# DeltaNet and SiLU feed-forward: chunk 0's keys read in runs of 16 tokens, their lengths computed by GpSimd, the diagonal blocks taken from PSUM

## The chip, the core and the metric

The kernel runs on one core of one Trainium2 chip. The metric is device time in microseconds (us) of one execution, from repeated runs. The core's engines have their own instruction queues, run in order: TensorE (PE, its weight loads PEld), VectorE (DVE), ScalarE (ACT), GpSimd (POOL) and SyncE (SP), which here issues most of the DMA transfers.

## The reference

A DeltaNet recurrence over 768 tokens for 4 x 8 heads of dimension 48, then a feed-forward block with SiLU. All data are float32.

```python
batch, n_heads, seq, head_dim = (4, 8, 768, 48)
n_tokens, d_model, d_ff = (3072, 384, 2048)

k_n = k / (np.linalg.norm(k, axis=-1, keepdims=True) + 1e-06)
for t in range(S):
    kt, vt, bt = (k_n[:, :, t], v[:, :, t], beta[:, :, t, None])
    y[:, :, t] = np.einsum('bhd,bhde->bhe', q[:, :, t], state)
    v_old = np.einsum('bhde,bhd->bhe', state, kt)
    state = state + bt[:, :, :, None] * np.einsum('bhd,bhe->bhde', kt, vt - v_old)

x = y.transpose(0, 2, 1, 3).reshape(B * S, H * D)
h = x @ w_in
out = (h * (1.0 / (1.0 + np.exp(-h)))) @ w_out
```

## The kernel before

The sequence is cut into `NCH` = 6 chunks of `C` = 128 tokens. In a chunk the recurrence is turned into matrix products: the keys' scores (k times k transposed) of each head form a strictly triangular matrix of 128 x 128, of which each half of 64 tokens is solved by itself; in a half the two diagonal blocks of `T` = 32 tokens are inverted on VectorE, 128 blocks at once (32 heads x 4 blocks, one to a partition), and the corners between the blocks are joined on TensorE. Chunk 0 inverts in two steps: `invert_first` inverts blocks of 16 (`Q`), and the first joins (`corner`, `turned`, `straight`) make blocks of 32 of them; `merge_half` makes 64. The feed-forward of one chunk fills TensorE while the next chunk's recurrence is worked on. Its weights come by SP in pieces (`fetch_w_in`, `fetch_w_out`) and are rearranged on ScalarE, VectorE and GpSimd (`narrow`). The order of the instructions on each engine is that of the program text: `pin` ties each instruction behind the one before on its engine, `in_line` does it for SP's DMAs. The interleaving after the start is written by hand as strings of letters (`script`, `chunks`); later loads start at counts of TensorE's work (`loads`).

What the change touches is the start, where no feed-forward work exists yet:

- Keys. `load_k(0)` reads chunk 0's keys into `kbufs[0]` by `load_pair`: one token to a partition, all heads of a batch along the free axis, each head in a slot of `W` = 64 of which `D` = 48 are filled; the rest is set to zero on VectorE (L207). There are six transfers (L144), in pieces of 48 floats.
- Lengths. GpSimd squares the keys (`square`, L385), VectorE adds them (`add_squares`, L389) and runs `norm_steps`: an integer seed for the reciprocal root, three Newton steps, then length `n`, its reciprocal and -beta/length^2 (`step`), transposed so that it stands by block (L403 to L426). GpSimd then writes the lengths in the order of the values (`n_slot`, L440 and L443) and `step` on the diagonal of x (L1493).
- Scores. `turn` transposes the keys of one batch on TensorE (L510) and copies them from PSUM to `turned_kq` by VectorE or ScalarE (L522, L524); `first_score` makes the scores of that batch (L539) and copies them to `ap` (L554 by ScalarE, L557 by VectorE).
- Diagonal blocks. `diagonal_blocks` copies the 32 x 32 blocks out of `ap` into `stage`, 32 partitions a copy (six by ScalarE, L554, two by GpSimd, L560); `turn_diagonal` transposes them on VectorE so that each block lies on one partition (L578). Then `invert_first` begins (L697), with pairs of instructions L705 and L709, and ends with the transpositions L716 and L720. The joins begin with `corner` (L743, emptied by L750).
- Fillers. `busy(n)` issues n matmuls whose results nothing reads (L347). In the inversion's loop they stand behind steps 9, 11, 13 and 14:

```python
    for n in range(Q):
        done = next(inv)
        if n in (9, 11, 13):
            busy(2 if n < 13 else 1, done, Sync)
        if n in (6, 8, 10, 12):
            turn(1, n // 2 - 3, 0, M)
        if n == 14:
            busy(1, done, Sync)
```

Other names: `z` (`zbuf`) first holds chunk 0's queries; `sums_of_w`, `sums_of_g` and `stage` are large tiles whose room several things use in turn; `vf` holds a chunk's values; L467 multiplies them by the lengths; `state` is the recurrence's state, still zero in chunk 0. Lines L832 are `merge_half`, L866 and L910 the first products behind the joins, L1088 the feed-forward's first matmul.

## Time and profile before

| | |
|---|---|
| median of 3 runs | 634.13 us (633.98 to 637.14) |
| the profiled execution's own time | 633.96 us |
| its span, from the first to the last instruction | 631.8 us |
| mean granted TensorE clock | 0.989 |

All positions are in us from the span's start; 2.2 us of the profiled execution lie outside the span. A row of a timeline gives start, duration, engine, line, operation, output and inputs, shape and count; in square brackets stands how long the engine had been idle and what released it. A row of a group gives busy time and the mean of one in ns, then the idle time ahead of it. DMA rows give the KB of one issue and the median us from issue to landing. The granted clock is the share of TensorE's full speed that the chip allowed.

### The profile page before, as it was taken

What the parts mean: (1) busy time and instruction counts of PE and PEld (TensorE: products, weight loads), DVE (VectorE), ACT (ScalarE), POOL (GpSimd) and SP (SyncE); (2) the same over time, 40 slices, a digit from 0 to 9 for tenths busy, and PEclk for the clock granted to TensorE, in tenths of its full rate; (3) what the DMA queues carried; (4) which work ended last, traced back from release to release, by engine and by line L of the source; (5) the groups of instructions that cost most, each with busy time, mean ns of one, the idle gap of its engine ahead of it and who ended that gap; (6) DMA issues with size and microseconds to landing.
All of it is one profiled execution on the core that took longest, in us unless ns stands there. A gap on an engine that the chain in (4) does not pass through costs nothing.

```text
span 631.8 us, 21374 instructions
## 1 busy us (share of the span) xinstructions
PE 617.7 (98%) x9390; PEld 543.3 (86%) x9390; DVE 415.5 (66%) x927; ACT 226.7 (36%) x516; POOL 94.0 (15%) x101
## 2 busy tenths in 40 slices
PE   8889989999999999999999999999999999999997
PEld 5578778666799989989989989989989989988997
DVE  6886779999667974546975554976444983345432
ACT  4657873332441122451122451122452122454210
POOL 5234631335020020020020010020002000000000
PEclk9869999999999999999999999999999999999999
DMA  9656506350459360459141359433254024010011
GB/s 175 134 141 199 170 16 149 116 86 4 101 100 186 62 108 4 95 107 188 34 92 20 72 125 156 65 75 44 52 113 95 2 75 62 17 38 1 0 26 26
DMA packets 136941, 52.61 MB, mean 83 GB/s; under 512 B 108672, under 2 KB 130432, under 8 KB 136848
## 3 DMA queue, kind: packets, MB, share of 16 engines
q1 hardware_dynamic: 136512, 51.09, 39.6%
q8 instruction: 74, 1.21, 0.9%
q10 hardware_dynamic: 336, 0.15, 0.1%
q14 instruction: 19, 0.16, 0.1%
HBM read 39.09 MB, written 9.96 MB: 78 GB/s over the span
## 4 chain that ended last, share of the span: by engine, by line
PE 93%; SPq 2%; DMA 1%; issue 1%; ACT 1%; DVE 0%
PE phid L1088 34%; PE px L1200 17%; PE py L1200 13%; PE po L1132 5%; PE pb_c L866 3%; PE pa L539 2%; SPq L144 2%; PE pb_c L1303 2%; PE pb_c L854 2%; PE pyc L945 2%; PE pc L1303 2%; PE pb_c L1132 2%; PE pb_c L886 2%; PE pa L1303 1%; PE pyc L932 1%; PE px L808 1%
## 5 line engine op out<-in xcount | busy, mean ns | idle before, releaser
L1088 PE MATMUL phid<-xT,w_in 128*128 128x256 f32 x960 | 214.9, 382 | 1.9 <-issue 1.7
L1088 PEld LDWEIGHTS phid<-xT,w_in 128*128 128x128 f32 x960 | 180.2, 190 | 26.9 <-issue 2.8
L1098 ACT ACTIVATE gT<-phid 128x512 f32<-128x512 f32 x72 | 42.9, 597 | 115.2 <-PE phid L1088 106.2
L656 DVE SCALAR_TENSOR_TENSOR rank<-g,step,x 128x31 f32<-128x31 f32 (+15 forms) x124 | 49.8, 402 | 23.3 <-DMA g<-blocks 19.8
L1200 PE MATMUL px<-sums_of_w,sums_of_g 128*128 128x192 f32 x320 | 56.6, 329 | 0.0
L1200 PE MATMUL py<-w_out,sums_of_g 128*128 128x192 f32 x320 | 56.2, 328 | 0.0
L1200 PEld LDWEIGHTS px<-sums_of_w,sums_of_g 128*128 128x128 f32 x320 | 52.2, 190 | 0.4
L1200 PEld LDWEIGHTS py<-w_out,sums_of_g 128*128 128x128 f32 x320 | 52.3, 190 | 0.3
L661 DVE TENSOR_TENSOR x<-x,rank 128x31 f32<-128x31 f32 (+15 forms) x124 | 42.5, 342 | 4.3
L477 POOL TENSOR_TENSOR vf<-vf,n_slot 128x768 f32<-128x768 f32 x10 | 14.8, 1492 | 175.4 <-DMA vf<-in_v_dram 129.9
L1183 DVE TENSOR_TENSOR sums_of_g<-gT 128x384 f32<-128x384 f32 (+1 forms) x48 | 24.6, 540 | 14.6 <-ACT gT L1098 14.5
L498 DVE STREAM_TRANSPOSE kq<-stage 128x512 f32<-128x512 f32 x28 | 28.4, 1121 | 6.8 <-DMA stage<-in_q_dram 3.5
L554 ACT COPY xT<-pyc 48x128 f32<-48x128 f32 (+2 forms) x120 | 31.1, 259 | 1.6
L1211 DVE TENSOR_TENSOR o<-o,kept 128x192 f32<-128x192 f32 (+1 forms) x29 | 11.5, 425 | 26.7 <-ACT kept L1208 26.7
L560 POOL COPY g<-x 64x256 f32<-64x256 f32 x4 | 5.0, 1244 | 150.8 <-DVE x L664 150.8
L891 DVE TENSOR_TENSOR state<-state,pb_c 128x384 f32<-128x384 f32 x22 | 11.2, 550 | 24.6 <-PE pb_c L886 24.6
L866 PEld LDWEIGHTS pb_c<-vf,xi 64*64 64x64 f32 x736 | 23.3, 138 | 3.2 <-issue 2.3
L866 PE MATMUL pb_c<-vf,xi 64*64 64x48 f32 x736 | 24.9, 223 | 0.1
L1132 PE MATMUL po<-w_out,gT 128*128 128x384 f32 x64 | 23.7, 491 | 0.0
L1200 PE MATMUL py<-w_out,gT 128*128 128x192 f32 x128 | 23.4, 331 | 0.0
L859 DVE TENSOR_TENSOR vf<-vf,pb_c 128x384 f32<-128x384 f32 x22 | 11.2, 550 | 18.3 <-PE pb_c L854 15.5
L1200 PE MATMUL px<-w_out,gT 128*128 128x192 f32 x128 | 22.4, 327 | 0.0
(293 smaller groups left out, 1094.5 us busy)
## 6 DMA issues: line engine op xcount, KB each, us to landing
vf<-in_v_dram SPq DMA_DIRECT2D x48, 96.0 KB, 2.8
out_dram<-o SPq DMA_DIRECT2D x42, 96.0 KB, 2.2
w_out<-in_moe_w_in_dram SPq DMA_DIRECT2D x4, 768.0 KB, 5.0
sums_of_w<-in_moe_w_out_dram SPq DMA_DIRECT2D x4, 768.0 KB, 4.6
kb<-in_k_dram SPq DMA_DIRECT2D x12, 192.0 KB, 4.5
kb<-in_k_dram SPq DMA_DIRECT2D x24, 96.0 KB, 4.0
raw<-in_moe_w_in_dram SPq DMA_DIRECT2D x3, 768.0 KB, 6.8
blocks<-ap SPq DMA_DIRECT2D x32, 64.0 KB, 1.9
```

Of the source, the lines that this page charges most:

```text
L477: pin(nc.gpsimd.tensor_tensor(out=vf, in0=vf, in1=of, op=ALU.mult))
L498: pin(nc.vector.transpose(out=kqs[c, b][:, :, j, :].rearrange("p a (i m) -> p a m i", i=T), in_=src.rearrange("p a (m d) -> p a m d", d=D) ...
L554: return pin(nc.scalar.copy(to, of))
L656: pin(nc.vector.scalar_tensor_tensor(out=tv, in0=g[:, 0:m, m : m + 1].to_broadcast([P, m, n]), scalar=step[:, m : m + 1], in1=x[:, m : m + ...
L661: yield pin(nc.vector.tensor_tensor(out=x[:, 0:m, m:T], in0=x[:, 0:m, m:T], in1=tv, op=ALU.add))
L866: yield pin(nc.tensor.matmul(pz[rows, n * D : (n + 1) * D], lhsT=xis[g][rows, u * H + 2 * p + e, :], rhs=vfs[c][rows, hf, g * HB + u, p, : ...
L1088: pin(nc.tensor.matmul(ph[:, j * GT : (j + 1) * GT], lhsT=w_in[:, a, (2 * f + j) * P : (2 * f + j + 1) * P], rhs=xTs[c, hf][:, a, :], star ...
L1098: pin(nc.scalar.activation(out=hidden_of(c, hf, f), in_=ph[:], func=ACTF.Silu, scale=-0.5 if in_blocks(c) else 0.5))
L1132: pin(nc.tensor.matmul(pos[i][:, 0:DM], lhsT=hidden_of(0, hf, f // 2)[:, at : at + C], rhs=w_outs[f // HFF][:, f % HFF, :], start=(f == 0) ...
L1183: pin(nc.vector.tensor_tensor(out=sums_of_g[:, k, fs], in0=of[0], in1=of[1], op=op))
L1200: pin(nc.tensor.matmul(to, lhsT=at, rhs=quarter(f, *b) if isinstance(b, tuple) else sums_of_w[b][:, f], start=start and f == 0, stop=f == ...
L1303: pin(nc.tensor.matmul(to[:, i * GT : (i + 1) * GT], lhsT=left(a, slice(f, f + 1))[:, 0], rhs=right(b), start=start and i == 0 and n == 0, ...
```

## The change

1. Chunk 0's keys are first read by two transfers into `stage`, with 16 consecutive tokens of a head to a partition, so that one piece is 16 x 48 floats. Transfer e brings the heads of parity e (16 pairs of batch and head pair, 8 blocks of tokens each). `pad` copies them on chip into `kbufs[0]` in slots of 64, the even heads by ScalarE and the odd ones by VectorE, in two halves.
2. Four `first_turn` transpose them and write them by VectorE (the first) or ScalarE (the others) to `turned_kq`, where a token's place is reached with a stride of 16 floats. `turned_kq` now has keys and queries apart. The scores of two batches share a pair of banks, and which half of a bank holds which tokens is exchanged for some heads, so that the scores come out in the places that they had.
3. The diagonal blocks are made straight from PSUM: ScalarE multiplies one half by a 0/1 column (`halves`), VectorE adds the other half times the other column. The copies to `ap` come behind them.
4. The squares are made by ScalarE (first half) and GpSimd (second half). The sums are brought to one block a partition by four matmuls with a selecting matrix (`sel`, built from `ident` on VectorE). The root and the square of the length are computed by GpSimd in 14 instructions, with two refinements in place of three; VectorE takes the reciprocal and multiplies by beta, which it has transposed. ScalarE writes `step` on the diagonal. The lengths in the order of the values are written after the inversion.
5. `load_k(0)` comes again, behind `load_v(0)`, and brings the keys by token, as the state update needs them. Half of beta's issues move from ScalarE's queue to SP's, and ScalarE's table load (Silu) ahead of its own. Some memsets move between engines. Three fillers at the start read zeros only and don't wait for `ident`; of the six in the inversion's loop two are left.

```diff
-    for t in (kbufs[0], zbuf, kbufs[1]):
+    keys_0 = stage[:, 2 * BH * T + 4 * P :].rearrange("p (e x) -> p e x", e=2)
+    padded_0 = kbufs[0][:].rearrange("p b a e w -> p (b a e w)").rearrange("p (s e w) -> p s e w", e=2, w=W)
+    halves = const.tile([P, 2], FP32, name="halves")
+    for t in (kbufs[0], zbuf):
...
-    for g in range(2):
-        load_k(0, slice(HB * g, HB * (g + 1)))
+    for e in range(2):
+        issue(
+            keys_0[:, e],
+            k.rearrange("b (a e) (c i s) d -> e c (b a) i (s d)", e=2, c=NCH, i=2 * NB)[e, 0],
+        )
+    pin(nc.scalar.activation(out=seen[:], in_=seen[:], func=ACTF.Silu))
...
+    def pad(h):
+        for e, by in enumerate((by_act, by_dve)):
+            done = by(padded_0[:, h * STEPS // 2 : (h + 1) * STEPS // 2, e, 0:D], half_of(h)[:, e])
+        return done
...
+    def first_turn(h, by):
+        pt = bank(M, "pt")
+        for i in range(4):
+            pin(nc.tensor.transpose(
+                pt[:, C * i : C * (i + 1)], padded_0[:, 4 * h + i].rearrange("p e w -> p (e w)"), ident[:]
+            ))
+        to = turned_kq[:, 0].rearrange("p b a (i s) -> p s (b a i)", s=STEPS)[:, 4 * h : 4 * h + 4]
...
+    def first_step():
+        po = bank(M, "po")
+        for i in range(2):
+            for e in range(2):
+                pin(nc.tensor.matmul(
+                    po[:, STEPS * i : STEPS * (i + 1)], lhsT=sel[:, e, i].rearrange("p j g n f -> p (j g n f)"),
+                    rhs=ss_0[:, e], start=e == 0, stop=e == 1,
+                ))
...
+        pin(nc.scalar.copy(ss, po[:, 0:T]))
+        pool, root = nc.gpsimd, seed.bitcast(FP32)
...
-    turned_kq = const.tile([P, B, 2, NP, C], FP32, name="kq")
+    turned_kq = const.tile([P, 2, B, NP, C], FP32, name="kq")
...
+        for e in range(2):
+            of = pa[e][:].rearrange("p (n t) -> p n t", t=W)
+            to = diagonals[0][:, HH * g + e : HH * (g + 1) : 2]
+            pin(nc.scalar.mul(to, of[:, :, 0:T], halves[:, 0:1]))
+            pin(nc.vector.scalar_tensor_tensor(
+                out=to, in0=of[:, :, T:W], scalar=halves[:, 1:2], in1=to, op0=ALU.mult, op1=ALU.add
+            ))
...
+    padded = [pad(h) for h in range(2)]
+    squares = [first_squares(0, nc.scalar), first_squares(1, nc.gpsimd, padded[1])]
...
+    first_turn(0, (by_dve,))
+    first_sums(0, squares[0])
+    first_turn(1, (by_act,))
+    first_turn(2, (by_act,))
+    first_sums(1, squares[1])
+    first_turn(3, (by_act,))
+    steps = first_step()
+    next(steps)
...
+    scores = first_score(0) + first_score(1)
+    turn_diagonal(0)
+    for i, (to, of) in enumerate(scores):
+        by_act(to, of)
...
     load_v(0)
+    load_k(0)
...
-        if n in (9, 11, 13):
-            busy(2 if n < 13 else 1, done, Sync)
+        if n == 9:
+            busy(2, done, Sync)
...
-        if n == 14:
-            busy(1, done, Sync)
     corner, turned, straight = next(inv)
+    next(steps, None)
```

VectorE ahead of the inversion; `L697` before and `L831` now is the inversion's first instruction. Before, the last steps of the lengths and the transposition of the diagonal blocks:

```order
L389 TENSOR_REDUCE ss<-sq 128x8
L403 TENSOR_SCALAR seed<-ss 128x32
...
L418 TENSOR_SCALAR n<-nt 128x32
L419 RECIPROCAL nr<-n 128x32
L420 TENSOR_TENSOR nt<-nr,beta_tok 128x32
L423 SCALAR_TENSOR_TENSOR nt<-nr,nt 128x32
L426 STREAM_TRANSPOSE step<-nt 128x32
L578 STREAM_TRANSPOSE sums_of_w<-stage 128x32x32
L697 TENSOR_TENSOR sums_of_w<-sums_of_w,step 128x2x16x16
```

Now:

```order
L447 TENSOR_REDUCE ss<-sq 128x2x8 x2
L1622 STREAM_TRANSPOSE stage<-beta_tok 128x32
L1597 SCALAR_TENSOR_TENSOR stage<-pa_232,halves,stage 128x8x32
L1597 SCALAR_TENSOR_TENSOR stage<-pb_c_73,halves,stage 128x8x32
L1597 SCALAR_TENSOR_TENSOR stage<-pa_271,halves,stage 128x8x32
L1597 SCALAR_TENSOR_TENSOR stage<-pb_c_74,halves,stage 128x8x32
L712 STREAM_TRANSPOSE sums_of_w<-stage 128x32x32
L508 RECIPROCAL nr<-seed 128x32
L509 SCALAR_TENSOR_TENSOR step<-nr,stage 128x32
L831 TENSOR_TENSOR sums_of_w<-sums_of_w,step 128x2x16x16
```

The root's steps are gone from VectorE, four fused multiply-adds from PSUM (`pa`, `pb_c` are banks) stand ahead of the transposition, and the reciprocal and one step behind it.

GpSimd from the squares on, before:

```order
L385 TENSOR_TENSOR sq<-kb_76 128x384 x4
L592 MEMSET sums_of_w 128x1024
L560 COPY stage<-ap_168 32x512 x2
L440 COPY n_slot<-n 64x2x8
L443 COPY n_slot<-n 64x8 x2
L440 COPY n_slot<-n 64x2x8
L443 COPY n_slot<-n 64x8 x2
L1493 COPY sums_of_w<-step 128x32
L1496 MEMSET xi 128x1024 x2
```

Now:

```order
L441 TENSOR_TENSOR sq<-stage 128x768
L726 MEMSET sums_of_w 128x1024
L1610 MEMSET xi 128x1024 x2
L488 TENSOR_SCALAR seed<-stage 128x32
...
L482 TENSOR_TENSOR seed<-n 128x32
L1624 MEMSET kb_77 128x32x16
L1624 MEMSET sums_of_g 128x32x16
L851 COPY sums_of_w<-pick 128x32x16
L523 COPY n_slot<-nt 64x2x8
```

The chain of the lengths (14 rows from the first L488 to the last L482, twelve left out) stands behind three memsets, and the copies of the lengths (`n_slot`) moved behind the inversion, of which L851 is part.

SP from chunk 0's values (`vf`) on, before and now:

```order
L292 DMA raw<-in_moe_w_in_dram 128x3x512
L198 DMA vf<-in_v_dram 64x8x48 x8
L292 DMA w_out_109<-in_moe_w_in_dram 128x3x512 x2
L144 DMA sums_of_g<-in_q_dram 128x8x48
L144 DMA sums_of_g<-in_q_dram 64x8x48 x2
```

```order
L303 DMA raw<-in_moe_w_in_dram 128x3x512
L198 DMA vf<-in_v_dram 64x8x48 x8
L144 DMA kb_76<-in_k_dram 128x8x48
L144 DMA kb_76<-in_k_dram 64x8x48 x2
L144 DMA kb_76<-in_k_dram 128x8x48
L144 DMA kb_76<-in_k_dram 64x8x48 x2
L303 DMA w_out_115<-in_moe_w_in_dram 128x3x512 x2
```

The second read of chunk 0's keys (`kb_76`, the tile `kbufs[0]`) stands between the values and the next pieces of the weights.

More of the change, by code (lines that the diff above doesn't have):

```diff
@@ L314 @@
     pin(nc.gpsimd.memset(states[0][:], 0.0))
+    zeros = states[0][:].rearrange("p u a w -> p (u a w)")
+    for _ in range(3):
+        done = pin(nc.tensor.matmul(
+            bank(CC, "pw")[:, 0:DM], lhsT=zeros[:, 0:P], rhs=zeros[:, 0:DM], start=True, stop=True
+        ))
+        tensor.append(done.ins.engine)
     make_identity(nc, ident[:])
@@ L435, in norm_steps @@
             ))
[L436 removed]
+        engine = nc.vector
         of = n[:].rearrange("p (n e) -> p e n", e=2)
@@ L1486 @@
     busy(4)
-    for _ in norm_steps(0):
-        pass
+    next(steps)
     first_queries(0)
@@ L1491 @@
     step = step_of[0]
-    of_step = blocks[0][2].rearrange("p s t -> p (s t)")[:, 0 : T * T : T + 1]
-    pin(nc.gpsimd.tensor_copy(out=of_step, in_=step[:]))
-    turn_diagonal(0)
-    for t in xis:
-        pin(nc.gpsimd.memset(t, 0.0))
     for c in range(1, NCH):
```

156 lines of the change are left out of this document (121 added, 35 removed).

## Prediction

> **What bounds the kernel now.** I read the page first, then the granted clock in 1 us stretches, then each engine's timeline of the first 35 us.
>
> ```profile
> span 631.8 us, 21374 instructions
> PE 617.7 (98%) x9390; PEld 543.3 (86%) x9390; DVE 415.5 (66%) x927; ACT 226.7 (36%) x516; POOL 94.0 (15%) x101
> PE 93%; SPq 2%; DMA 1%; issue 1%; ACT 1%; DVE 0%
> ```
>
> TensorE is the bound over the span as a whole. The edit touches only the stage before about 31 us. From some 40 us on TensorE has no gaps to give back, so what the first stage gains or loses passes to the end as it is. What ends last in that stage is VectorE's chain (its timeline):
>
> ```profile
> 15.45 0.35 DVE L419 RECIPROCAL nr<-n 128x32 f32<-128x32 f32 x1
> 16.54 1.98 DVE L578 STREAM_TRANSPOSE sums_of_w<-stage 128x1024 f32<-128x1024 f32 x1
> 18.55 0.69 DVE L697 TENSOR_TENSOR sums_of_w<-sums_of_w,step 128x512 f32<-128x512 f32 x1
> 28.92 1.95 DVE L720 STREAM_TRANSPOSE sums_of_w<-sums_of_w 128x1024 f32<-128x1024 f32 x1
> ```
>
> The end of the key lengths (the reciprocal L419 and three small steps behind it) and the transposition of the diagonal blocks (L578) run one after the other. The inversion starts at 18.55, ends at 30.87 with L720, and TensorE's first joining matmuls wait for exactly that:
>
> ```profile
> 12.30 3.75 ACT L554 COPY stage<-ap 32x512 f32<-32x512 f32 x6
> 31.16 0.11 PEld L743 LDWEIGHTS pl<-sums_of_w,ap 32*32 32x32 f32 x2 [0.55 <-DVE sums_of_w L720]
> ```
>
> ScalarE's six diagonal copies end at 16.05, so both inputs of the inversion are ready at about 16.5: removing only one of the two chains would have brought nothing. The clock, in stretches of 1 us (busy time and instructions of each engine, then the granted clock, the share of the DMA engines, GB/s):
>
> ```profile
> 18.00:19.00 1.00, 0.56 (x5) 0.34 (x4) 0.96 (x2) 0.95 (x6) 0.74 (x1) 0.83 0.66 116
> 22.00:23.00 1.00, 1.00 (x9) 0.79 (x7) 0.90 (x4) 0.37 (x1) 0.00 (x0) 0.96 1.01 392
> 35.00:36.00 1.00, 0.07 (x3) 0.08 (x4) 0.95 (x3) 0.54 (x2) 0.00 (x0) 0.87 0.89 307
> 39.00:40.00 1.00, 0.51 (x21) 0.51 (x20) 0.72 (x2) 1.00 (x2) 0.20 (x1) 0.50 0.94 293
> 45.00:46.00 1.00, 1.00 (x44) 1.00 (x36) 0.98 (x2) 0.39 (x1) 0.00 (x0) 0.51 0.08 16
> ```
>
> From the fractions 0.83, 0.96, 0.87 and 0.51 the half clock holds from 18.66 to 22.08 and from 35.74 to 45.98: 3.4 us, and 10.2 = 3 x 3.4. So the clock moves in steps of 3.4 us, and the joins run half warm, half cold.
>
> **The change part by part, against the profiled run (633.96; the median of the three runs is 634.13, 0.17 above).** Times from the span's start.
>
> *Keys.* Six small issues give way to two transfers of 384 KB.
>
> ```profile
> 0.80 4.76 SPq L144 DMA_DIRECT2D kb<-in_k_dram  x6
> 6.23 1.61 POOL L385 TENSOR_TENSOR sq<-kb 128x384 f32<-128x384 f32 x2 [1.95 <-DMA kb<-in_k_dram]
> 9.00 1.61 POOL L385 TENSOR_TENSOR sq<-kb 128x384 f32<-128x384 f32 x2 [1.15 <-DMA kb<-in_k_dram]
> w_out<-in_moe_w_in_dram SPq DMA_DIRECT2D x4, 768.0 KB, 5.0
> ```
>
> Before, half of the keys were in by 6.2 and the rest by 9.0. Both new transfers are 768 KB together, for which the nearest row has 5.0 from issue: 1.3 + 5.0 = 6.3 at the latest; at the earliest the first half's 6.2 less the two issues that it waited for and that are saved (0.79 each), 4.6. I take 5.9, near the row of the same size. So the start is not much earlier; what is won is that all keys are there, not half.
>
> *Padding, squares, transposes.* The prices:
>
> ```profile
> 0.96 0.55 DVE L207 MEMSET kb<- 128x256 f32 x2
> L443 DVE COPY n_slot<-n 64x8 f32<-64x8 f32 x20 | 2.7, 175 | 0.1
> L557 DVE COPY g<-x 64x768 f32<-64x768 f32 x4 | 3.4, 840 | 0.1
> L389 DVE TENSOR_REDUCE ss<-sq 128x8 f32<-128x384 f32 x12 | 6.5, 548 | 5.5 <-POOL sq L385 5.5
> L522 DVE COPY kq<-pt 128x512 f32<-128x512 f32 x4 | 2.7, 686 | 1.4 <-PE pt L510 1.4
> L524 ACT COPY kq<-pt 128x512 f32<-128x512 f32 x2 | 1.2, 587 | 3.3 <-PE pt L510 3.3
> L477 POOL TENSOR_TENSOR vf<-vf,n_slot 128x768 f32<-128x768 f32 x10 | 14.8, 1492 | 175.4 <-DMA vf<-in_v_dram 129.9
> 16.89 1.84 POOL L1496 MEMSET xi<- 128x1024 f32 x2
> 2.39 4.21 PE L347 MATMUL pb_c<-state,ident 128*128 128x384 f32 x6 [2.39 <-POOL ident masks.py:199]
> 6.39 1.91 PE L510 MATMUL pt<-ident,kb 128*128 128x128 f32 x8
> ```
>
> Three fillers of zeros (4.2 us, L347) start near 1.4 instead of 2.4 and end before the keys are in. Ahead of the keys VectorE now builds `halves` and `sel`: from 0.96, four half-memsets (1.1), eight tiny ones (an estimated 0.1 each, 0.8), one of 512 (0.55), twelve small copies (12 x 0.175 = 2.1): 5.5, hidden by 0.4 under the keys. If that cover is gone, each 0.1 is lost in full. Padding is 384 elements a copy, 0.42 by the half of 0.840: first half padded at 6.35, second at 6.8. The transposes go at 1.91/8 = 0.24 each while cold, in two banks: turn 0 ends at 7.4, VectorE empties it by 8.3 (0.69 and the wait), turn 1 is emptied by ScalarE at 9.2, turns 2 and 3 at 10.1 and 10.7 (0.59 each). Beside that: GpSimd's squares 6.85 to 8.35 (1.49), VectorE's two sums of 768 (twice 0.548 each) 8.3 to 10.4, four selecting matmuls and the beta transpose to 11.1. GpSimd then does three memsets of 1024 elements (L592 and L1496 of before), ending at 8.35 + 3 x 0.95 = 11.2.
>
> *Scores and diagonal blocks.* 64 matmuls as before, but in one run.
>
> ```profile
> 10.00:11.00 1.00, 1.00 (x62) 0.89 (x63) 1.00 (x3) 0.73 (x2) 1.00 (x2) 1.00 1.49 163
> L554 ACT COPY ap<-pa 128x256 f32<-128x256 f32 x24 | 9.0, 375 | 7.7 <-PE pb_c L539 7.5
> L549 DVE TENSOR_TENSOR ap<-pb_c,above 128x256 f32<-128x256 f32 x20 | 8.3, 415 | 0.0
> ```
>
> TensorE issues 62 in a us: 11.1 to 12.2. ScalarE's scaled copy (0.375) of the first bank ends at 12.2; VectorE's four fused adds, priced as its products of 256 elements from PSUM and SBUF (0.415 and some 0.03 between), end at 14.0; the transposition (1.98) at 16.0. That replaces 3.75 us of ScalarE and 2 GpSimd copies. The plain copies of the scores follow behind on ScalarE, off the path.
>
> *Lengths by GpSimd.* Fourteen dependent steps of 32 elements, which no row of before shows on that engine.
>
> ```profile
> L385 POOL TENSOR_TENSOR z<-kb 128x384 f32<-128x384 f32 x12 | 9.5, 827 | 0.2
> L443 POOL COPY n_slot<-n 64x8 f32<-64x8 f32 x4 | 0.6, 186 | 0.1
> ```
>
> 1492 for 768 and 827 for 384 give 0.16 + 32 x 0.0017 = 0.22, with a dependence perhaps 0.30; ends 0.19 (the copies of 8) and 0.45 (twice 0.22). I take 0.30: 11.4 + 14 x 0.30 = 15.6, hidden by 0.4 under the transposition that ends at 16.0. Then the reciprocal (0.35) and one fused step (0.2), which stood ahead of L578 before: inversion at 16.6 instead of 18.55. I count **-1.8**, rounding for waits.
>
> *What moves behind.* The keys are read again, by token, six issues behind `load_v(0)`.
>
> ```profile
> 19.79 6.51 SPq L198 DMA_DIRECT2D vf<-in_v_dram  x8
> 33.12 4.36 SPq L292 DMA_DIRECT2D w_out<-in_moe_w_in_dram  x2
> ```
>
> SP is idle from 26.3 to 33.1; six issues at 0.79 fit (4.8 us), and their first reader is the state update behind the joins. Zero; if they were late, the two weight fetches queued behind them on SP are late by as much, up to 1.5 us. The value sizes on GpSimd start after the inversion instead of before it: six copies at 0.19, 1.1 us, ahead of a memset and the scaling of the values, which nothing reads before the joins are done: zero.
>
> *Fewer filler matmuls.* In the inversion two stay of six.
>
> ```profile
> 31.16:35.74 4.58, 3.48 (x262) 3.14 (x261) 3.31 (x8) 2.56 (x6) 2.72 (x2) 1.00 0.30 68
> 36.00:38.00 2.00, 2.00 (x121) 2.00 (x124) 1.93 (x4) 0.62 (x2) 0.63 (x1) 0.50 0.54 203
> 28.05 1.46 PE L347 MATMUL pb_c<-state,ident 128*128 128x384 f32 x4
> ```
>
> Four at 0.73 (1.46 for two) leave TensorE, 2.9 us of the five before the joins. They cost nothing there and their removal brings nothing, but the 3.4 us step before the joins is then about half empty, like that before 18.66 and that before 35.74, and both were followed by the half clock. I expect the joins' first 4.6 us (31.16 to 35.74) cold as well. Warm, their 262 matmuls take 3.48, 13.3 ns each; the cold stretch beside it has 121 in 2.0, 16.5 ns: 262 x 3.2 ns = 0.8, partly under the emptying copies. Bounds 0 and +3.5 (all of it at half speed); I take **+0.7**, near the cold row.
> The Trainium skill (TensorE: Matmul & The Clock Gate, What's actually happening) has the clock halve after a whole idle window of about 3.4 us. By that rule alone, with transposes left inside the window, the joins would stay warm and the sum would be 632.2; the half-busy stretches above speak for the earlier drop.
>
> Sum: 633.96 - 1.8 + 0.7 = 632.9.
>
> **Rivals.**
> *Cold and longer (slower than before).* TensorE is so empty before the joins that they run cold throughout and the clock comes back one step later, because the dense matmuls just miss a step's start (39:40 above, half empty, did not bring it back). Price: 2.1 for the joins (between 0.7 and 3.5) and 1.7 (half of 3.4) for the step: 633.96 - 1.8 + 2.1 + 1.7 = 636.0. It decides if the clock returns at 49 or later. For it: the removed fillers. Against: everything dense also starts earlier.
> *Warm sooner.* The same steps, the other way: the clock is back at 42.6 instead of 45.98, and the joins lose nothing: 633.96 - 1.8 - 1.7 = 630.5.
> *Strided emptying.* The turned keys are now written with a stride of 64 bytes.
>
> ```profile
> L560 POOL COPY g<-x 64x256 f32<-64x256 f32 x4 | 5.0, 1244 | 150.8 <-DVE x L664 150.8
> ```
>
> GpSimd pays 4.9 ns an element for a strided read here, while VectorE's g<-x of 768 takes 1.09 with the same stride; for strided writes only the transpositions bear (1.98 for 1024, 1.93 ns). At that rate each of the four emptyings takes 0.4 more, three on the path: the gain falls to 0.6, 634.1. The Trainium skill (SBUF — State Buffer, Door 1: The DMA port swizzle) says that accesses crossing to a new 16-byte line pay; VectorE's row disagrees for reads, none shows a write.
> *GpSimd late.* At 0.45 a step the lengths come at 17.7, 1.7 after the transposition: 634.6. This is also the case in which the edit doesn't bring its point.
>
> **How the numbers follow.** Forecast 0.38, warm sooner 0.20, cold and longer 0.19, strided 0.11, GpSimd late 0.12. Predicted 632.9. The range takes in warm sooner with keys at 5.4 (630.0) and cold and longer (636.0). Under 0.5% (3.2 us) a measurement of this kernel can hardly tell from no change: faster than 631.0 is most of warm sooner and the edge of the forecast, 0.19; slower than 637.3 only the tail of cold and longer, 0.08; within, 0.73.
>
> **What would show it.** Right: the keys land by 6, the inversion's first TENSOR_TENSOR at 16.6, GpSimd's last step before the end of the transposition, the joins' first weight load near 29.3 at clock 0.5. Wrong: an inversion start above 18 (keys, strided emptying or GpSimd: each has its own row), a granted clock of 1 through 29 to 35, or a gap on TensorE after 45 that waits for the second read of the keys.

## The result and the profile after

The changed kernel is slower: 637.9 us median of 15 runs (635.87 to 639.74) against 633.98 of 15 runs before, ratio 1.0051, 95% interval 1.0035 to 1.0067. The same two kernels run again gave 637.38 against 634.15, ratio 1.0052 (1.0033 to 1.0070). I had forecast 632.9 and a range that ended at 636.0.

The profiled execution took 636.48 us. First VectorE's timeline: start, duration, line, operation, out<-in, and in brackets the idle time ahead and what ended it.

```profile
7.46 0.63 DVE L691 COPY kb<-stage 128x384 f32<-128x384 f32 x2 [3.12 <-DMA stage<-in_k_dram]
8.68 1.03 DVE L691 COPY kq<-pt 128x512 f32<-128x512 f32 x1 [0.51 <-PE pt L455]
16.28 0.48 DVE L1597 SCALAR_TENSOR_TENSOR stage<-pb_c,halves,stage 128x256 f32<-128x256 f32 x1
16.79 1.98 DVE L712 STREAM_TRANSPOSE sums_of_w<-stage 128x1024 f32<-128x1024 f32 x1
18.68 0.30 DVE L508 RECIPROCAL nr<-seed 128x32 f32<-128x32 f32 x1
19.24 0.69 DVE L831 TENSOR_TENSOR sums_of_w<-sums_of_w,step 128x512 f32<-128x512 f32 x1
```

The second key transfer lands at 7.46, not 5.9. The emptying of the turned keys takes 1.03, not 0.69. The inversion starts at 19.24: 0.69 later than the 18.55 of before, where I had 16.6. The lateness against my sum grew on the way: 1.1 at the start of the first emptying (8.68, I had 7.6), 2.2 at the end of the last one (12.88 against 10.7), 2.8 at that of the fused adds (16.76 against 14.0), 2.6 at the inversion. ScalarE's and GpSimd's rows:

```profile
10.98 1.90 ACT L688 COPY kq<-pt 128x512 f32<-128x512 f32 x2 [0.39 <-PE pt L455]
14.44 0.47 ACT L1596 ACTIVATE stage<-pa,halves 128x256 f32<-128x256 f32 x1 [0.90 <-PE pb_c L1591]
17.68 0.24 POOL L482 TENSOR_TENSOR seed<-n 128x32 f32<-128x32 f32 x1
```

Two emptyings take 1.90 on ScalarE (0.587 each before), a scaled copy 0.47. GpSimd's last step ends at 17.9, under VectorE's transposition, which ends at 18.77. TensorE's timeline, then its clock in 1 us stretches (the columns are busy time and instructions of PE, PEld, DVE, ACT and POOL, then granted clock, DMA share, GB/s):

```profile
1.38 3.99 PE L328 MATMUL pb_c<-state 128*128 128x384 f32 x6 [1.38 <-POOL state L325]
7.97 1.52 PE L455 MATMUL pt<-ident,kb 128*128 128x128 f32 x8 [2.61 <-DVE kb L691]
9.85 1.94 PE L455 MATMUL pt<-ident,kb 128*128 128x128 f32 x8 [0.36 <-DVE kq L691]
```

```profile
8.00:9.00 1.00, 1.00 (x7) 1.00 (x8) 0.49 (x3) 0.31 (x1) 0.77 (x1) 0.71 0.04 4
11.00:12.00 1.00, 0.79 (x4) 0.39 (x2) 0.34 (x1) 1.00 (x2) 1.00 (x2) 0.58 0.94 161
35.00:36.00 1.00, 0.60 (x61) 0.50 (x47) 0.96 (x2) 0.77 (x3) 0.54 (x1) 0.87 0.51 84
49.00:50.00 1.00, 1.00 (x32) 0.77 (x34) 0.14 (x1) 0.85 (x2) 1.00 (x1) 0.81 0.78 145
```

TensorE waits 2.61 us for the keys. Right behind that the clock is halved, from 8.4 to 11.8: one step of 3.4. It is halved again from 35.74, as before, but up to 49.38: four steps instead of three. In all 19 traces, up to 70 us, the clock fell behind 3.4 us in which TensorE was busy for 20 to 97%, never wholly idle, and came back behind 3.4 us with 88 to 100%.

The joins now have three gaps; before they had two. TensorE's timeline, rows after an "issue" gap, in which it waited for nothing that the profile shows; before, then after:

```profile
35.93 0.26 PE L832 MATMUL py<-xe_y,ap 32*32 32x32 f32 x1 [1.13 <-issue]
39.49 0.21 PE L832 MATMUL px<-xi,xe_y 32*32 32x32 f32 x1 [1.14 <-issue]
```

```profile
29.94 0.20 PE L877 MATMUL pl<-sums_of_w,ap 32*32 32x16 f32 x2
...
33.84 0.18 PE L893 MATMUL pl<-sums_of_w 32*32 32x32 f32 x1 [1.29 <-issue]
37.29 0.20 PE L966 MATMUL py<-xe_y,ap 32*32 32x32 f32 x1 [1.69 <-issue]
41.14 0.26 PE L966 MATMUL px<-xi,xe_y 32*32 32x32 f32 x1 [1.42 <-issue]
```

The joins start 1.2 us earlier (29.94 against 31.16). They need only the first of the two transpositions that end the inversion. VectorE's timeline, before and then after:

```profile
28.01 1.06 DVE L716 STREAM_TRANSPOSE sums_of_w<-sums_of_w 128x512 f32<-128x512 f32 x1
```

```profile
28.72 1.09 DVE L850 STREAM_TRANSPOSE sums_of_w<-sums_of_w 128x512 f32<-128x512 f32 x1
29.65 1.96 DVE L854 STREAM_TRANSPOSE sums_of_w<-sums_of_w 128x1024 f32<-128x1024 f32 x1
```

The first matmuls behind the joins that work on the values (L866 before, L1000 after; "state matmuls" below) come at 42.88 instead of 41.23. The profiled execution's 2.52 us more are made up so: 0.69 by the inversion's start, 0.96 between there and the state matmuls, 0.80 up to the feed-forward's first matmul (49.31 before, 51.76 after), and 0.07 behind it. It was one of the changed kernel's shorter executions, 1.4 under the median, while the one profiled before lay at its kernel's median; so these 2.52 us are not all of the 3.2 to 3.9 by which the medians differ.

Counting TensorE's matmuls up to each gap shows what the gaps are (stretches from 0 to the gap's end, before and then after):

```profile
0.00:35.92 35.92, 29.49 (x601) 20.76 (x601) 27.07 (x78) 20.18 (x44) 14.99 (x36) 0.95 0.79 146
0.00:39.48 39.48, 31.92 (x728) 23.05 (x729) 30.48 (x84) 22.22 (x49) 16.82 (x37) 0.91 0.78 150
```

```profile
0.00:33.83 33.83, 25.48 (x472) 17.71 (x473) 23.33 (x78) 20.88 (x44) 14.61 (x45) 0.95 0.85 167
0.00:37.28 37.28, 27.24 (x600) 19.37 (x601) 25.92 (x84) 22.32 (x48) 16.31 (x46) 0.93 0.82 166
0.00:41.13 41.13, 29.67 (x728) 21.67 (x728) 29.08 (x89) 24.70 (x54) 18.14 (x47) 0.89 0.80 166
```

472, 600 and 728: the gaps lie exactly 128 matmuls apart, each with its weight load. One packet of 16 KB on the queue that the profile names "instruction" belongs to each: it shows at 31.0, 34.9 and 38.4, 1.1 us behind the first use of the piece before, and each gap ends 2.4 to 2.8 us behind its packet. Between two gaps' ends lie 3.45 to 3.85 us, while the 128 matmuls between them take 1.76 (33.84 to 35.60) at full clock. So in the joins TensorE is paced by the arrival of its program. That the count decides, and not the work that stands there, shows in the three kernels below with 20 or 24 more matmuls ahead of the joins: their gaps again end at 600 and 728, so 20 or 24 matmuls earlier within the joins. Before, the packet for matmul 472 came at 29.0, 2 us ahead of the joins' start; after, it came at 31.0, 1.1 us behind it. I put that down to the fillers, which held TensorE while its queue was read on.

### The profile page after: what moved, and what is told of

Its sections match the earlier page's. It is cut to its first block, busy times and chain, and to the rows that moved or that the text cites. A ratio compares the mean times of both kernels' runs of the same rounds, so it can differ in the third digit from the quotient of the medians.

```text
span 634.8 us, 21390 instructions
## 1 busy us (share of the span) xinstructions
PE 617.3 (97%) x9390; PEld 543.2 (86%) x9390; DVE 414.2 (65%) x932; ACT 229.0 (36%) x520; POOL 95.6 (15%) x111
## 4 chain that ended last, share of the span: by engine, by line
PE 95%; ACT 2%; issue 1%; DMA 1%; DVE 0%; SPq 0%
PE phid L1222 33%; PE px L1334 17%; PE py L1334 13%; PE po L1266 5%; PE pb_c L1000 3%; PE pa L672 3%; PE pb_c L988 2%; PE pb_c L1437 2%; PE pyc L1079 2%; PE pc L1437 2%; PE pb_c L1266 2%; PE pb_c L1020 2%; PE pa L1437 1%; PE pyc L1066 1%; PE px L942 1%
## 5 line engine op out<-in xcount | busy, mean ns | idle before, releaser
L1000 PEld LDWEIGHTS pb_c<-vf,xi 64*64 64x64 f32 x736 | 23.4, 138 | 3.2 <-issue 2.3
L1000 PE MATMUL pb_c<-vf,xi 64*64 64x48 f32 x736 | 25.1, 223 | 0.1
```

Source lines behind the costliest of these rows:

```text
L1000: yield pin(nc.tensor.matmul(pz[rows, n * D : (n + 1) * D], lhsT=xis[g][rows, u * H + 2 * p + e, :], rhs=vfs[c][rows, hf, g * HB + u, p, : ...
```

## The experiments

Times are medians; each ratio is to runs of the kernel before made beside them. The sets go by question, not by order. Times of single steps are from one profiled execution each. In 13 traces whose program has the same length ahead of the joins, the stretch from the feed-forward's first matmul to the end took 581.4 to 584.6 us, and in a fourteenth, an execution of 641.82, it took 589.5: one trace's end is uncertain by that much.

**First set: one suspect at a time.** Before, plus the second read of the keys:

```diff
+    load_k(0)      # behind load_v(0), kernel before
```

> The kernel before with one thing added: chunk 0's keys are fetched a second time, by token, right behind load_v(0), as the changed kernel does; nobody needs the second copy before the first state update at about 66 us. Theory R (the second fetch is what costs: its 192-byte pieces run at 27 to 34 us, when the DMA engines were empty before, and hold up the fetching of TensorE's instructions): the gaps that end the joins' rows as 'issue' grow from 1.13 + 1.14 us to about 4, and the time is 1.5 to 3 us over before (635.5 to 637). Theory F (the removed fillers: TensorE reaches the short joining matmuls without a queue of instructions behind it): gaps and time as before, within 0.5 us.

635.53 against 634.52, ratio 1.0015 (0.9995 to 1.0036). The gaps:

```profile
35.69 0.26 PE L832 MATMUL py<-xe_y,ap 32*32 32x32 f32 x1 [2.20 <-issue]
39.53 0.21 PE L832 MATMUL px<-xi,xe_y 32*32 32x32 f32 x1 [1.41 <-issue]
```

They grew by 1.34, but the joins had started 1.7 earlier (29.48) and the gaps ended where they had ended before. Their packets showed 0.7 and 0.5 earlier than before (32.5 and 36.8 against 33.2 and 37.2), so here a packet took some 0.5 longer to the end of its gap; that much of theory R stays possible. A cost of the second read of up to 2.3 us lies in the interval and is not shown.

```diff
-    load_k(0)
+        (WINDOW + PACKET * 7 + -14, load_k, 0),      # in the paced loads
```

> The changed kernel with the second fetch of the keys moved out of the joins, into the paced loads behind the weights. Theory R: the three issue gaps of 1.29, 1.69 and 1.42 us shrink to about 1 + 1, the first state weights are multiplied 1.5 us earlier, and with luck the clock returns a step of 3.4 us earlier: 633.5 to 635 against 636.5 of the changed kernel. Theory F: no change, 636 to 638. Rival S (strided emptying and late keys alone set the end, through the inversion's start at 19.2): no change.

637.46, ratio 1.0040 (1.0016 to 1.0064), level with the changed kernel: three gaps again (0.96, 1.62, 1.41), the first although the DMA engines were 0.02 busy from 30 to 35. Theory R fell as the main cause. The trace showed something that I had not asked for: through the whole key stage matmuls ran at half speed (eight transposes 1.94, a score 0.31 instead of 0.22), though the granted clock's row reads 1.00 there, and the inversion started at 22.3. The first eight transposes were among the slow ones; whether the clock had risen at all before them the trace doesn't tell.

```diff
-            one(to[:, part], of[:, part])
+            one(to[:, part].rearrange("p s n -> p n s"), of[:, part].rearrange("p s n -> p n s"))
```

> The changed kernel with the emptying of the turned keys written in another order: four tokens next to each other (16 bytes) at a time, so the strided side is the read from PSUM. Theory S (the writes at a stride of 64 bytes set the 1.03 and 1.05 us of each emptying where 0.69 and 0.59 stood for contiguous ones): each takes 0.6 to 0.75, the scores and the inversion start 0.9 to 1.2 us earlier (18.0 to 18.3 instead of 19.24); the end follows by 0 to 1.2 us, since the clock's steps may swallow it. Rival: the strided read of PSUM costs as much, no change.

VectorE's and ScalarE's timelines:

```profile
8.52 0.69 DVE L691 COPY kq<-pt 128x512 f32<-128x512 f32 x1 [0.47 <-PE pt L455]
...
20.71 0.69 DVE L831 TENSOR_TENSOR sums_of_w<-sums_of_w,step 128x512 f32<-128x512 f32 x1
```

```profile
8.95 0.59 ACT L688 COPY kq<-pt 128x512 f32<-128x512 f32 x1 [0.77 <-PE pt L455]
```

The rate was as expected: 0.69 and 0.59, what contiguous emptyings took before. The stride of the write costs 0.34 on VectorE and 0.46 on ScalarE for 512 elements; a stride on the PSUM read, here of 512 bytes, costs nothing that shows. The end did not follow: 638.07, ratio 1.0047 (1.0024 to 1.0071). This execution too ran its key stage at half clock, from 9.6 to 19.9, and the inversion started at 20.7.

```diff
-        if n == 9:
-            busy(2, done, Sync)
+        if n in (9, 11, 13):
+            busy(2 if n < 13 else 1, done, Sync)
+        if n == 14:
+            busy(1, done, Sync)      # n == 14: after the turn, as before
```

> The changed kernel with the six filler groups of the inversion loop put back as before. Theory F (the removed fillers): two gaps instead of three before the first state weights, the joins at full clock, 1.5 to 2.5 us faster than the changed kernel (634 to 635). Theory R: the gaps stay at about 4.4 us together, and only the 0.3 us by which the first joining product came earlier is lost again: 636 to 637.5.

643.05, ratio 1.0124 (1.0085 to 1.0162): 5 us worse, against both theories. In the trace the gap at matmul 472 is gone, as theory F had it, and those at 600 and 728 are 1.10 and 1.74. But the fillers held the joins up: they began at 36.24, against 33.09 with the late second read, where the inversion had begun at the same 22.3. It also adds 8 matmuls ahead of the joins, which the next set shows to matter by itself.

**Second set: the pieces of the program, and the clock.**

```diff
+    for _ in range(10):      # behind the three wide ones at the start; 32 columns each
+        done = pin(nc.tensor.matmul(
+            bank(CC, "pw")[:, 0:T], lhsT=zeros[:, 0:P], rhs=zeros[:, 0:T], start=True, stop=True
+        ))
...
```

> The changed kernel with ten small matmuls of zeros (32 columns each, some 0.3 us together) behind the three wide ones at the start, where TensorE waits for the keys anyway. Every gap of TensorE in the joins lies an exact multiple of 128 matmuls from the next (after matmuls 472, 600 and 728 in the traces), and each ends 2.3 to 3.2 us after a 16 KB packet of its program. Theory P (TensorE's program comes in pieces of 128 matmuls, a piece is asked for when the one before it is begun, and takes some 3.7 us; in the changed kernel the first of these boundaries lies 4 matmuls behind the start of the joins, in the kernel before it was passed 2 to 3 us earlier since fillers were running): the small matmuls move the boundaries 20 matmuls forward, the piece is asked for before the joins start, the first gap goes and the first state matmuls come about 1.5 us earlier; time 1 to 2 us under the changed kernel's 637.9, if the clock's steps do not hide it. Rival R (the gaps come from the second read of the keys that runs beside them): three gaps as before, same time.

645.3, ratio 1.0183 (1.0155 to 1.0211). Each of the ten counts as two matmuls in the trace; they took not 0.3 us but 2.9, up to 8.25, and so filled the wait for the keys. The boundary at matmul 472 was passed without a gap, as theory P said; the next was worse than any before (TensorE's and SP's timelines):

```profile
40.35 0.26 PE L911 MATMUL pl<-sums_of_w 32*32 32x32 f32 x2 [3.60 <-issue]
```

```profile
34.14 7.77 SPq L303 DMA_DIRECT2D w_out<-in_moe_w_in_dram  x2
```

The packet for it shows at 37.9, 4 us behind the first use of the piece before, at the end of a weight transfer during which the core moved 354 GB/s (36 to 38). The loads are spaced by counts of instructions (`PACKET` = 256 is 128 matmuls and their weight loads). That the packet waited for the weights is my reading of this one trace; in the two other kernels with 20 and 24 more matmuls it came ahead of them (35.3 and 35.0), and the gap was 0.87 and 0.65.

```diff
     busy(3)
+    busy(10, wide=32)      # kernel before
```

> A control: the kernel before, with ten small matmuls of zeros behind the wide ones at the start, which moves the pieces of TensorE's program by 20 matmuls against all later work, as in the changed kernel with the same addition (which lost 7 us by it). Theory A (where the pieces' boundaries fall against dense stretches and paced loads is a property of this kernel's order, so any such shift costs): 638 to 642. Rival (only the changed kernel's second read collides with the moved pieces): 633.5 to 635.

644.99, ratio 1.0158 (1.0124 to 1.0192), above even what theory A gave. So this cost belongs to the kernel's order, not to the change: ten small matmuls cost 11 us. Not all of it is the shift, for here they were not in idle time: they ran up to 8.47 and held up the transposes (8.31 instead of 6.39), and the inversion began 1.3 later. 4 of the 11 us are there by the feed-forward's first matmul (53.2), and the rest comes later: from 300 to 450 us TensorE was busy 146.91 instead of 149.77, and the clock was halved once more, from 439.4 to 446.2. Why is not shown; the kernels with 8, 20 and 24 more matmuls also have a gap of 1.0 to 1.2 ahead of the state matmuls, which fits no multiple of 128. The change itself leaves the matmuls ahead of the joins at 340, as before.

```diff
-    for _ in range(3):
+    for _ in range(5):      # the wide matmuls of zeros at the start
```

> The changed kernel with five wide matmuls of zeros at the start instead of three, so that TensorE is busy up to 8.0 us instead of 5.4. Theory C (the wait of 2.5 to 3 us for the keys is what drops the clock to one half at 8 to 11 us, in most runs for three steps of 3.4 us: transposes 1.94 us, the four summing matmuls 1.89 and scores 3.7 us where the warm ones take 1.1, 1.06 and 2): no half clock before the inversion, which starts at 18.2 to 18.6 in every run; time 2 to 3 us under the changed kernel, 635 to 636. Rival: the clock falls anyway, since TensorE waits for the emptying copies between the transposes (half-busy window): no change.

638.8, ratio 1.0078 (1.0054 to 1.0102). The time is not decisive, since the edit moves the pieces by 4 matmuls. But the trace speaks against theory C. TensorE's timeline and its clock:

```profile
1.38 5.84 PE L328 MATMUL pb_c<-state 128*128 128x384 f32 x10 [1.38 <-POOL state L325]
7.71 1.06 PE L455 MATMUL pt<-ident,kb 128*128 128x128 f32 x8 [0.49 <-DVE kb L691]
```

```profile
13.00:14.00 1.00, 1.00 (x52) 1.00 (x47) 0.01 (x1) 0.00 (x0) 0.83 (x4) 0.50 0.93 307
```

TensorE stood idle for only 0.49 ahead of the keys, and the clock fell all the same, from 13.0 to 16.4; the inversion started at 19.6. In the run with ten small matmuls there was no wait at all, and it fell from 10.0 to 20.2. That leaves the rival, the waits between the groups of transposes, which no run settles. The four edits together:

> Four edits to the changed kernel together: five wide matmuls of zeros and ten small ones at the start, the emptying of the turned keys in pieces of four tokens, and the second read of the keys behind the weights. If theories C, P and S hold, the inversion starts at 17.3 to 17.9, the joins have two gaps and the time is 632 to 634, level with the kernel before or 1 us under it. If the clock falls all the same: 635 to 637.

643.32, ratio 1.0159 (1.0121 to 1.0196): the shift by 24 matmuls covers all else. The added ones also ran past the keys, up to 9.9, and the clock fell at 14.0, again without a wait.

**Third set: the keys' landing, with the program's length kept.**

```diff
-    for e in range(2):
-        issue(keys_0[:, e], ...[e, 0])
+    for h in range(2):
+        for e in range(2):
+            part = slice(h * STEPS // 2 * D, (h + 1) * STEPS // 2 * D)
+            issue(keys_0[:, e, part], ...[e, 0][:, :, part])
```

> The changed kernel with its two key transfers cut into four, the first eight steps of both parities first (runs of 1.5 KB). If the bytes set the landing, the first half of the steps is whole at 5.2 and its padding, transposes and squares start 2 us earlier, while TensorE never waits 2.6 us: inversion at 18 to 18.5, 635 to 636.5. If a transfer's fixed time and its 384 pieces set it, the last quarter lands later (8 to 8.5) and the gain is under 0.5 us.

635.01, ratio 1.0014 (0.9996 to 1.0033): of some 3.3 us that the change costs, 2.4 are back, and the interval lies below that of the result (1.0035 to 1.0067). VectorE's timeline, then TensorE's gaps:

```profile
4.72 0.36 DVE L693 COPY kb<-stage 128x384 f32<-128x384 f32 x1 [0.37 <-DMA stage<-in_k_dram]
6.29 0.36 DVE L693 COPY kb<-stage 128x384 f32<-128x384 f32 x1 [1.20 <-DMA stage<-in_k_dram]
...
16.73 0.69 DVE L833 TENSOR_TENSOR sums_of_w<-sums_of_w,step 128x512 f32<-128x512 f32 x1
```

```profile
31.44 0.18 PE L895 MATMUL pl<-sums_of_w 32*32 32x32 f32 x1 [1.42 <-issue]
35.16 0.21 PE L968 MATMUL py<-xe_y,ap 32*32 32x32 f32 x1 [1.90 <-issue]
38.46 0.25 PE L968 MATMUL px<-xi,xe_y 32*32 32x32 f32 x1 [0.87 <-issue]
```

The last quarter lands at 6.29, TensorE doesn't wait for the first, the key stage stays at full clock, and the inversion starts at 16.73: near the prediction's 16.6, 1.8 ahead of the kernel before. But the state matmuls come at 40.4, only 0.9 ahead. Three gaps hold the joins, and the clock is halved from 32.9 to 46.6: four steps where before had three.

On top of it, the second read moved as in the run above; then the piecewise emptying as well:

> The kernel with four key transfers, and the second read of the keys moved from the joins into the paced loads behind the weights. With four transfers the inversion started at 16.7, 1.8 us before that of the kernel before, but the first state matmuls came only 0.9 earlier and the end 0.5 later. Theory R (the second read, with DMA engines 0.9 busy from 26 to 32 us, delays the fetches of TensorE's program): the first gap (1.42) and the second (1.90) lose about 1 us together, 633 to 634. Theory P (pieces of 128 matmuls, each some 3.6 us from request to use, whatever else the DMA engines do): the gaps stay within 0.3 us, time 634.5 to 635.5.

> The same as the run before it in this list, with the turned keys also emptied in pieces of four tokens (0.59 and 0.69 an emptying instead of 1.0 in the traces). The inversion should start at 15.6 to 16.0. If the joins hang on the inversion's end, the first state matmuls come another 0.8 us earlier: 632 to 633.5. If the clock's steps or the program's pieces decide, 0 to 0.3 us.

They took 634.56, ratio 1.0015 (0.9990 to 1.0040), and 633.67, ratio 1.0004 (0.9984 to 1.0024). In the first the gap of 1.42 fell to 0.41, the others were 1.60 and 1.14; no gain in time shows. Its key stage was cold again (half clock from 10.6 to 17.4, inversion at 19.4), so four transfers don't always keep it warm. The second is the best median of all and level with the kernel before. Its inversion was not seen at 15.6 to 16.0: the profiled execution was its slowest, 641.82, with half clock from 10.3 to 17.2 and the inversion at 18.8.

```diff
-    for _ in range(3):        # 384 columns each
+    for _ in range(2):        # 512 columns each
-    busy(4)
+    busy(3, wide=512)
+        if n == 13:
+            busy(1, done, Sync)
+        if n == 14:
+            busy(1, done, Sync)
```

> The kernel with four key transfers, and two wide matmuls of zeros back in the inversion's last steps, paid for by one fewer at the start and one fewer before the inversion (512 columns instead of 384 each), so that TensorE's program ahead of the joins is as long as it was and its pieces stand where they stood. Theory P: the wide matmuls let the sequencer run ahead, the piece at matmul 472 is asked for before the joins start, the first gap (1.42) shrinks to under 0.5 and the first state matmuls come up to 0.7 us earlier: 634 to 635. Rival (only the joins' start counts): they start 0.7 to 1.4 us later and all is later by that: 635.5 to 636.5.

634.62, ratio 1.0020 (0.9997 to 1.0042). The gaps were 0.80, 1.69 and 1.14. As theory P said, the first shrank, and the state matmuls came 23.1 us behind the inversion's start instead of 23.6; but the joins started 1.4 later (28.88), and the time is within the scatter of the run without fillers.

**Fourth set: the clock in the key stage, with the program's length kept.** The changed kernel unchanged, once more:

> The changed kernel itself once more, for a second profile beside those that follow. Theory C (TensorE's wait for the keys drops the clock, and how long it stays down hangs on where the 3.4 us steps fall): half clock somewhere between 7 and 20 us, for one to three steps, and an inversion that starts between 19.2 and 22.3; 636.5 to 639. Rival: the first profile's one cold step is the rule, inversion at 19.2 again.

637.38. Its inversion and its clock:

```profile
21.39 0.69 DVE L831 TENSOR_TENSOR sums_of_w<-sums_of_w,step 128x512 f32<-128x512 f32 x1
```

```profile
9.00:10.00 1.00, 0.51 (x3) 0.54 (x4) 1.00 (x2) 0.79 (x1) 1.00 (x2) 0.53 0.73 144
19.00:20.00 1.00, 1.00 (x5) 0.73 (x4) 1.00 (x1) 1.00 (x3) 0.30 (x1) 0.85 0.34 61
```

Half clock from 9.06 to 19.3, three steps of 3.4; the inversion is 2.15 later than in the first profile. Yet its time, 636.39, equals the first profile's 636.48: the state matmuls were 2.2 later, the feed-forward's first matmul 1.4, the end none.

```diff
-            bank(CC, "pw")[:, 0:DM], lhsT=zeros[:, 0:P], rhs=zeros[:, 0:DM], ...
+            bank(CC, "pw")[:, 0:512], lhsT=zeros[:, 0:P], rhs=zeros[:, 0:512], ...
     first_turn(1, (by_act,))
+    busy(1)
     ...
     first_turn(3, (by_act,))
+    busy(1)
-    busy(4)
+    busy(2)
```

> The changed kernel with the three wide matmuls at the start 512 columns wide instead of 384, and two of the four wide ones ahead of the inversion moved to behind the second and the fourth group of turned keys. TensorE's program ahead of the joins is exactly as long as before, so its pieces stay where they were. Theory C: no or one cold step in the key stage, inversion at 18.3 to 19.2; 1 to 2 us under the changed kernel in the same rounds. Rival (cold or warm, the joins and the clock after them set the end): within 0.5 us of it.

636.02, ratio 1.0037 (1.0018 to 1.0057), 1.4 under the changed kernel in the same rounds. One cold step was left (8.0 to 11.4), as in the first profile, and the inversion started at 20.0, later than theory C's 18.3 to 19.2; the added matmuls (1.5 and 0.8) stand ahead of the later groups. The time has theory C's sign and size, but not by its path, and the two intervals overlap, so it is not shown.

The two combinations, in which the kernel with four transfers, piecewise emptying and late second read keeps its key stage warm:

> Four key transfers, emptying in pieces of four tokens, the second read behind the weights, and two of the four wide matmuls ahead of the inversion moved into the key stage; program as long as before. Theory C: key stage warm, inversion at 15.8 to 16.5 in the profile. If the end follows the inversion from there, 631.5 to 633; if the joins are held by the pieces of the program (3.6 us each from the joins' start), 632.5 to 634.

> The same with the two wide matmuls that are left ahead of the inversion moved into its last steps, as the kernel before had them. Theory P: the first piece of the joins' program is asked for ahead of their start, no first gap, state matmuls up to 0.7 us earlier than in the run before: 631.5 to 633. Rival: the joins start later by the 0.7 us that the last wide matmul takes, and so does all else: 633 to 634.5.

635.88, ratio 1.0020 (0.9999 to 1.0040), and 635.65, ratio 1.0028 (1.0007 to 1.0049). The first's key stage was warm and its inversion began at 16.4, but the joins began only at 29.17, 2.3 behind the end of the transposition that they need: ahead of them in TensorE's queue stood chunk 1's turned keys (TensorE's timeline, first row):

```profile
28.10 1.15 PE L645 MATMUL pt<-ident,kb 128*128 128x128 f32 x8 [0.68 <-ACT stage L659]
29.17 0.20 PE L879 MATMUL pl<-sums_of_w,ap 32*32 32x16 f32 x2
```

An inversion that starts this early is no longer what ends last: TensorE's own queue is, here at half clock from 17.4 to 24.2. The second had no first gap, as theory P has it, but the joins at 31.3. And the last combination:

> Four key transfers, emptying in pieces of four tokens, second read of the keys behind the weights, and two wide matmuls in the inversion's last steps with the program ahead of the joins as long as before. If the gains add up (each was 0.3 to 1 us beside the four transfers alone): 632 to 633.5, level with the kernel before or a little under it. If the joins' three pieces of program and the clock's steps set the end whatever comes before, 633.5 to 635.5 as in its parts.

635.46, ratio 1.0022 (1.0001 to 1.0042), so the gains did not add up. The profiled execution shows what they could be at best: inversion at 16.7, no gap at 472, half clock for three steps (32.9 to 43.1), the state matmuls at 39.4, 1.9 ahead of the kernel before. It took 632.29, the shortest of its twelve and 3.2 under their median. No version beat the kernel before.

## Why the prediction was wrong

The sum was -1.8 for the inversion's start and +0.7 for cold joins. Both terms failed, and a premise under them.

- *Keys* ("I take 5.9"). The second transfer landed at 7.15 to 7.64 in nine traces. The row of 5.0 us is that of one transfer of 768 KB; here the second half of the bytes, issued at 1.55, took 5.9 by itself. Beta's small pieces ran beside it; no run tells what they cost. It put the chain 1.1 late by itself, and it is the term whose mending showed in the time: with four transfers the inversion came at 16.73 and 2.4 us came back. How much of that is the landing, and how much the warm key stage that came with it, is not separated.
- *Emptying*. Priced as contiguous, 0.69 and 0.59; measured 1.03 and 0.95 to 1.05. With the waits between them the emptyings made the chain another 1.1 late. The strided rival was right on this row. The Trainium skill (SBUF — State Buffer, Door 1: The DMA port swizzle) has accesses pay for each new 16-byte line; emptying by four floats, 16 bytes, took 0.69 and 0.59, which agrees with it.
- *Scores* ("64 matmuls" at 62 a us, 1.1). The 62 of that row are passes: each of these matmuls shows as two in the trace, so there are 128, and they took 2.1 (13.2 to 15.3). With a scaled copy of 0.47 instead of 0.375 this added the last 0.6.
- *The clock in the key stage*. I priced the transposes cold, and the selecting matmuls and the scores warm. That held in the first profile (one cold step, up to 11.8). But in all nine traces of kernels with two transfers part of the key stage ran at half speed, for one to four steps, with the inversion at 19.2 to 22.3. The idle 2.6 us ahead of the keys are not needed for it: in three of the nine TensorE had 0.5 us of idle time there or none, and the clock fell too. What it costs at the end stays unsure: the second profile of the changed kernel, cold for three steps, was no slower than the first.
- *Second read, "zero"*. Neither shown wrong nor right: the one run that isolates it gave +1.0 us with an interval that holds zero; taking it out of the joins changed nothing that can be measured.
- *Joins, +0.7 for a cold start*. They were not cold from their start; the clock fell at 35.74, as before. What they lost were gaps: without fillers ahead of them the piece at matmul 472 was asked for 2 us later. The size was near (0.96) by luck; the mechanism was another.
- *Premise: "what the first stage gains or loses passes to the end as it is", and the joins "wait for exactly" L720*. The joins' first matmuls need only the transposition ahead of it (L716, 28.01 to 29.07); until 31.16 they stood behind fillers. And from the joins on the program's pieces set the pace. With four transfers an inversion 1.8 earlier made the state matmuls 0.9 earlier and the end nothing. This step would have failed even with every term ahead of it right.
- *Right*: GpSimd's chain hidden under the transposition (0.33 a step instead of 0.30); and the rival "cold and longer" on its deciding sign: the clock returned at 49.38. Its way there was another, gaps in the program's supply, and its price of 636.0 was 1.9 under the median.
- *Luck*: the inversion at 16.73 with four transfers, where I had 16.6. Half of the keys were there at 4.7 and the transposes ran warm, which made up for emptyings of 1.01.

What stays open is the clock's share. Around the joins, 14 of the other 18 traces had four steps, among them that of the kernel before with only a second read, so the fourth step needs no change of the keys. The record of all runs goes further: over 127 runs of the kernel before, the granted clock had a mean of 0.990; 51 of them had 0.992, with a median time of 633.2, and 39 had 0.989, with 634.7. One step of 3.4 us at half clock is 0.0027 of the span, so that is one step and 1.5 us. Over the 27 runs of the changed kernel the mean was 0.984, about two steps more, and none reached 0.990. By that the clock could make up most of the loss. It is not shown: within the changed kernel time and granted clock don't go together (10 runs at 0.981 had a median of 637.5, 6 at 0.989 had 638.3), and the clock's row can miss a cold start, as the run with the late second read showed.

## What to carry to other kernels

Before pricing an earlier start, count what the stage behind it is paced by: here short matmuls ran faster than their program arrived, and an inversion 1.8 us earlier gained nothing at the end. When a kernel's loads are spaced by instruction counts, keep the count in every experiment; ten small matmuls cost 7 to 11 us and hid the effects under test. And when data come in fewer, larger transfers, price the landing of the last one by a row of the same issue, not of the same bytes, and look at how the densest engine is busied around it: it ran at half clock for part of that stage in nine traces of nine, with and without a wait.

## What the hardware showed

TensorE's program arrives in pieces of 128 matmuls with their weight loads, 16 KB, with 3.45 to 3.85 us from one piece's first use to the next's in the joins; a dense run of 13 ns matmuls uses a piece up in 1.76 us. In one trace, with a weight transfer at 354 GB/s ahead of the packet, a gap was 3.6 us. TensorE's clock fell behind stretches of 3.4 us in which it was 20 to 97% busy. Writing 512 floats to SBUF at a stride of 64 bytes took 1.03 us on VectorE and 1.05 on ScalarE, against 0.69 and 0.59 in groups of four floats with the stride moved to the PSUM read.
